# The last attention unit in one tile shape: scores and side products as four products of 64 rows by 32 columns

## The chip, the cores and the metric

One NeuronCore of one Trainium2 chip. The metric is device time in microseconds (us) of one execution; the profile gives one execution, instruction by instruction. TensorE is PE in the profile, its weight loads are PEld; VectorE is DVE, ScalarE is ACT, GpSimd is POOL, SyncE is SP.

## The reference

A transformer block whose layer norms are modulated by a condition vector: 2048 tokens of width 512, attention with 32 heads of width 16 that share one key head and one value head, then a bilinear feed-forward part of width 1792. All in float32.

```python
mod = (silu(c) @ w_mod).reshape(1, 6, 1, 512)
sa, ca, ga, sb, cb, gb = (mod[:, i] for i in range(6))
h = layernorm(x) * (1 + ca) + sa
q, k, v = heads(h @ wq), h @ wk, h @ wv
p = softmax(q @ k.T * 16 ** -0.5)
x = x + ga * (merge(p @ v) @ wo)
h = layernorm(x) * (1 + cb) + sb
x = x + gb * (((h @ w_gate) * (h @ w_up)) @ w_down)
```

## The kernel before

Large products are made of float16 halves: a float32 operand is split into a high and a low part, and three products (high-high, low-high, high-low, `TERMS` in line 487) accumulate in PSUM.

The attention runs in `NU` = 32 units (8 slices of 256 tokens by 4 groups of 8 heads). A unit has `KT` = 16 tiles of 128 keys, and each of them is one turn of `attend` (line 1314). In a turn PE does four score products, each with 51 rows in the array: `qk_exp` (line 667) multiplies a key tile (51 rows by 128 columns, the weights) with 512 columns of queries. `a` says which half of the array's rows is used (0 to 50 or 64 to 114), `p` which two heads. ACT then takes the exponential of each score bank into a tile P. The last score product of a turn may be issued as two of 256 columns (line 680). At the end of a turn `pv` (line 707) multiplies the P tiles of an earlier turn with the values: 32 columns of weights for each of four heads, so that four products stand side by side in the array's columns. For most key tiles P is float32 and the product is issued as two instructions; for three of 16 key tiles (`F16_AT`, line 53) P is split into float16 halves and there are three terms.

In units 0 to 30 `pv` uses all 128 rows. In unit 31 (`NU - 1`) it uses the array's row halves apart, each with an accumulator of its own (lines 716 to 719), so its products are 64 rows by 32 columns, eight side by side; `pv_out` (line 736) adds the two accumulators. `pv` lags by a turn, so the first two turns of unit 31 end with the 128-row `pv` of unit 30.

The turn's remaining array time is filled with halves of other products. A `Group` (line 499) is one PSUM bank that accumulates `n` products of 128 rows; `half` issues one 64-row half of a product, `whole` (used after the last unit) all 128 rows. With two operands (gate and up weights, 256 columns each, `ffn_work` line 918) the second part of a half is kept in `pending`, and `flush` (line 494) issues it after the next score or maximum. While one row half of the array does a score (512 columns), the other does such a side half (256 and 256 columns, or 512 in a down projection). The order in a turn is written out by hand:

```python
MANY = "x1 e0 x1 m0 x1 e0 x1 e0 x1 m0 x1 m0 x1 m0 x1 e0"
```

`x` is a side half, `e` a score, `m` a row maximum's product (`max_mm`, line 600) for a later unit; the digit is the row half and changes with the turn. The maxima are done ahead, and in unit 31 none is left: there `m` is a side half of a second group (line 1358). A side group whose row half changes waits for an exponential of the turn before (lines 534 to 535, `sync`): the first side half of each turn waits for ACT so. After unit 31 come its last `pv`, the normalisation, the output projection and what is left of the feed-forward work, with 128-row products.

Of the kernel before, what the change touches and what calls it, by code (L numbers as in the profile page):

```python
# [23 lines left out]
ST = 256  # L24
NS = S // ST
NC = KC
NU = NS * NC
# [23 lines left out]
Q_BURSTS = {26: 3, 27: 3, 28: 3, 29: 3}  # L51
F16_FROM = 10
F16_AT = ((0, 5, 10), (0,), (0, 5, 10), (0, 5, 10))
P_SHIFT = float(14 * np.log(2.0))

LOW = -3.0e38
SYNC = mybir.DependencyInfo(mybir.DependencyClass.Sync, mybir.DependencyReason.DATA)
# [11 lines left out]
def adaln_mqa_glu_kernel(ctx: ExitStack, tc: tile.TileContext, x_in, wq_in, wk_in, wv_in, wo_in,  # L69
                         wg_in, wu_in, wd_in, c_in, wm_in, out):  # L70
    nc = tc.nc
# [13 lines left out]
    def ps_hold(name="side", shape=(128, 512)):  # L85

        tag, bufs = pool.popleft()
        t = psum.tile(list(shape), F32, name=name, tag=tag, bufs=bufs)
        held[id(t)] = (t, tag, bufs)
        return t  # L90
# [5 lines left out]
    def ps_mx(name="mx", shape=(128, 512)):  # L96
        t = ps_hold(name, shape)
        ps_give(t)
        return t

    def ps_sc():
        return ps_mx("sc")
# [49 lines left out]
    for i in range(3):  # L152
        t = consts.tile([128, 2, 2, ST], F16, name=f"sst{i}")
# [9 lines left out]
    rows = consts.tile([128, 3], F32, name="rows")  # L163
    prow = consts.tile([128, 2], F32, name="prow")
    nc.gpsimd.tensor_tensor(prow[:, 0:1], ident[:, 50:51], ident[:, 114:115], op=OP.add)
    nc.gpsimd.tensor_scalar(prow[:, 1:2], prow[:, 0:1], -P_SHIFT / 32.0, 0.0, op0=OP.mult, op1=OP.add)
    nc.gpsimd.tensor_scalar(prow[:, 0:1], prow[:, 0:1], P_SHIFT / 32.0, 0.0, op0=OP.mult, op1=OP.add)
    nc.gpsimd.memset(sst[2], 0.0)
# [180 lines left out]
    for k in range(KC):  # L349
        for j in range(4):  # L350
            nc.tensor.matmul(pmA[32 * j:32 * j + 32, 0:256], silr[:, k, 0:32], wmA[:, k, 256 * j:256 * j + 256],
                             start=(k == 0), stop=(k == KC - 1))
# [33 lines left out]
    nc.gpsimd.memset(tok, 0.0)  # L386
    kts16 = sorted({k for ks in F16_AT for k in ks})
    v16 = consts.tile([128, 2, len(kts16), 32], F16, name="v16")
# [102 lines left out]
    sync = {"due": False, "exp": None, "before": None, "half": None, "early": False}  # L491
    pending = []

    def flush():
        for f in pending:
            sync.update(due=True, half=f().ins.name)
        pending.clear()

    class Group:

# [5 lines left out]
        def put(self, r0, r1):  # L506
            if self.p is None:
                if self.prepare:
                    self.prepare()
                self.p = ps_hold("side")  # L510
            terms = self.op(self.did[r0])
            start = sum(self.did) == 0
            for r in range(r0, r1):
                self.did[r] += 1
            stop, rows, w = self.ended(), slice(64 * r0, 64 * r1), BT // len(terms)

            def part(c):
                left, right = terms[c]
                return nc.tensor.matmul(self.p[:, c * w:(c + 1) * w], left[rows], right[rows],  # L519
                                        start=start and c == 0, stop=stop and c == len(terms) - 1)  # L520

            if len(terms) > 1 and r1 - r0 == 1:
                pending.append(lambda: part(1))
                return part(0)
            return [part(c) for c in range(len(terms))][0]
# [5 lines left out]
        def half(self, r):  # L531

            mm = self.put(r, r + 1)
            if self.rows not in (None, r):
                tc.add_manual_dep(mm.ins, sync["before"], SYNC)
            self.rows, self.turn = r, now[0]
            sync.update(due=True, half=mm.ins.name)
            if self.ended():
                ended.append(self)

# [61 lines left out]
    def max_mm(u, a, op):  # L602
        kind, p, t, kc = op
        s = sst[u % 3]
        m = ps_sc() if kind == "diff" else ps_mx()
        keys = [kst[:, kc * 512:(kc + 1) * 512]]
        if kind == "diff":
            keys = [kng, kst[:, (kc + 1) * 512:(kc + 2) * 512]]
        for i, w in enumerate(keys):
            nc.tensor.matmul(m, s[64 * a:64 * a + 48, t // 2, p, t % 2 * 128:(t % 2 + 1) * 128], w[64 * a:64 * a + 48, :],  # L610
                             start=(i == 0), stop=(i == len(keys) - 1))
        part = mparts[u][:, a, 4 * (t // 2) + 2 * p + t % 2, kc:kc + 1]
        if kind == "one":
            nc.vector.tensor_reduce(part, m, axis=AX.X, op=OP.max)  # L614
        elif kind == "diff":
            r = rel[a] = work.tile([128, 512], F32, name="rel", tag="x1", bufs=6)
            relus.append(lambda: nc.scalar.activation(r, m, AF.Relu))
        else:
            nc.vector.tensor_tensor_reduce(out=rel[a], in0=m, in1=rel[a], scale=1.0, scalar=LOW, op0=OP.add,
                                           op1=OP.max, accum_out=part)  # L620
# [34 lines left out]
    pd = {}  # L655
    f16s = [KT * u + k for u in range(F16_FROM, NU) for k in F16_AT[u % NC]]
    assert f16s[0] % KT == 0
# [9 lines left out]
    def qk_exp(u, kt, p, a, last=False):  # L667
        s = sst[u % 3]
        v = u * KT + kt
        if v in f16_set:  # L670
            ptl[u, kt, p, a] = p_sets[f16_set[v]][0][:, 2 * a + p]
        else:
            ptl[u, kt, p, a] = work.tile([128, D], F32, name="P", tag="P", bufs=8)
        t = ps_sc()
        keys = kst[64 * a:64 * a + 51, kt * 128:(kt + 1) * 128]
        if pending and last:
            for c in range(2):
                if c:
                    flush()
                nc.tensor.matmul(t[:, c * ST:(c + 1) * ST], keys, s[64 * a:64 * a + 51, c, p, :], start=True, stop=True)  # L680
        else:
            nc.tensor.matmul(t.rearrange("k (c n) -> k c n", c=2), keys, s[64 * a:64 * a + 51, :, p, :],  # L682
                             start=True, stop=True)
        if last and sync["early"]:
            ex = nc.scalar.activation(tok[:, 1:2], tok[:, 0:1], AF.Copy)  # L685
            tc.add_manual_dep(ex.ins, sync["half"], SYNC)
            sync.update(due=False, exp=ex.ins.name)
        ex = nc.scalar.activation(ptl[u, kt, p, a], t, AF.Exp)  # L688
        if sync["due"]:
            sync.update(due=False, exp=ex.ins.name)  # L690
# [518 lines left out]
    NSTEP = 32  # L1209
# [12 lines left out]
    def max_half(a):  # L1222
        n = mstep[a]
        mstep[a] += 1
        if n >= len(flat):
            return
        u, i, last, ops = flat[n]
        max_parts(u)
        for kind, p, t, kc in ops[a]:
            max_mm(u, a, (kind, p, t, kc))  # L1230
        if mstep[1 - a] <= n:
            return
        u, i, last, ops = flat[n]
        if 0 < u < NU - 1 and i == QPRE:
            load_q(u + 1)
        if i == 12:
            max_parts(u + 1)
        if last:
            max_fin(u)
            (_, f, g), = max_rows(u)  # L1240
            later[min(mstep) + 1] = (f, g)
# [13 lines left out]
    now = [0]  # L1255
# [58 lines left out]
    def attend(u, kt):  # L1314
# [28 lines left out]
        for turn in range(2):  # L1343
# [5 lines left out]
            for j, (what, a) in enumerate(order):  # L1349
                if j == len(order) // 2:  # L1350
                    drain_posts()
                    if style is not NO_SIDE:
                        late_max()
                    hooks(u, 2 * (kt + turn))
                    for vj in f16_split.get(u * KT + kt + turn, ()):
                        p_split(*vj)
                a = a if style is NO_SIDE else a ^ turn
                if what == "m" and mstep[a] >= len(flat) and style is MANY:
                    mstep[a] += 1
                    side_half(a, second)  # L1360
                elif what == "m":
                    max_half(a)
                    drain_relus()
                elif what == "v":
                    end_turn(kt + turn)
                elif what == "x":
                    side_half(a)
                    continue
                else:
                    k = count[a] = count.get(a, -1) + 1  # L1370
                    qk_exp(u, kt + (k // 2 if style is MANY else turn), k % 2, a, j == len(order) - 1)
                flush()
# [48 lines left out]
    for g in begun:  # L1421
        for r in range(2):
            while g.did[r] < g.did[1 - r]:
                g.half(r)
                flush()
# [54 lines left out]
```

## Time and profile before

| what | us |
|---|---|
| median of 3 runs | 1639.53 (1637.69 to 1640.58) |
| the profiled execution | 1641.03 |
| its span, first to last instruction | 1639.1 |
| PE busy in the span | 1619.2 (99%) |
| unit 31, first side product to last `pv` | 1480.1 to 1526.7 |

The span is what the traces show; the profiled execution's time is 1.9 us longer, for what lies around it. Starts are us from the span's first instruction. Matmuls are pipelined: a row's duration is longer than the spacing of products that follow each other, so array time is read from starts.

### The profile page before, as it was taken

To read this page: it belongs to the slowest core of one execution; us is meant where nothing else is said; L and a number is where in the kernel's file an instruction comes from. 1 tells how busy PE (TensorE), PEld (TensorE's weight loads), DVE (VectorE), ACT (ScalarE), POOL (GpSimd) and SP (SyncE) were. 2 spreads that over 40 slices of the span, in tenths; PEclk is the share of its full clock that TensorE was granted. 3 is DMA by queue.
4 is the path that set the end of the run, shared out by engine and by line. 5 is a ranking of instruction groups with operands and counts; after the bars stand their busy time and mean duration, and the time that the engine had idled before them with its cause. 6 is when DMAs were issued, how large, how long until landed. Compare 5 with 4: busy or idle time off the path is not lost.

```text
span 1639.1 us, 41286 instructions
## 1 busy us (share of the span) xinstructions
PE 1619.2 (99%) x15993; PEld 747.7 (46%) x15993; DVE 1401.2 (85%) x2434; ACT 1220.8 (74%) x2421; POOL 955.7 (58%) x1316
## 2 busy tenths in 40 slices
PE   9999999999999999999999999999999999999998
PEld 4332333355533555335543455434545345444776
DVE  8999999889999999999999999999999999980211
ACT  6688878888777788778877788777877778877300
POOL 6857537875755566636656466653657556565422
PEclk9899999999999999999999999999999999999999
DMA  7213313342221000100011001100001001100100
GB/s 257 93 57 101 94 63 115 95 125 90 64 70 28 21 20 26 39 32 20 13 32 35 20 19 33 32 26 26 20 25 33 24 18 33 32 15 22 34 14 14
DMA packets 78996, 79.15 MB, mean 48 GB/s; under 512 B 30408, under 2 KB 59340, under 8 KB 78800
## 3 DMA queue, kind: packets, MB, share of 16 engines
q1 hardware_dynamic: 77744, 76.46, 14.9%
q8 instruction: 125, 2.05, 0.5%
q14 instruction: 71, 0.58, 0.1%
q10 hardware_dynamic: 1056, 0.07, 0.0%
HBM read 56.04 MB, written 17.05 MB: 45 GB/s over the span
## 4 chain that ended last, share of the span: by engine, by line
PE 92%; DVE 2%; POOL 2%; ACT 2%; DMA 1%; issue 1%; SPq 0%; POOLq 0%; ACTq 0%; DVEq 0%
PE side L519 41%; PE pv L728 29%; PE mx L610 8%; PE sc L682 8%; PE sc L680 3%; DVE mpart L614 2%; ACT P L688 1%; DMA wmA<-in_w_mod_dram 0%; PE pk L298 0%; PE sc L278 0%; PE part L290 0%; PE mxt L638 0%; DMA kwb<-in_B_w_down_dram 0%; PE sc L610 0%; POOL wg L1175 0%
## 5 line engine op out<-in xcount | busy, mean ns | idle before, releaser
L614 DVE TENSOR_REDUCE mpart<-mx 128x1 f32<-128x512 f32 x2016 | 1272.2, 683 | 83.8 <-PE mx L610 75.7
L688 ACT ACTIVATE P<-sc 128x512 f32<-128x512 f32 x1824 | 982.3, 599 | 219.9 <-PE sc L682 177.7
L610 PE MATMUL mx<-kst,sst 48*128 48x512 f16 x2032 | 628.8, 377 | 3.9 <-ACT P L688 2.6
L682 PE MATMUL sc<-sst,kst 51*128 51x512 f16 x1792 | 597.7, 379 | 0.8 <-ACT P L688 0.3
L519 PE MATMUL side<-h2T,wg 64*128 64x256 f16 (+1 forms) x2396 | 540.5, 271 | 0.6 <-POOL h2T L902 0.3
L519 PE MATMUL side<-h2T,wu 64*128 64x256 f16 (+1 forms) x2396 | 538.2, 270 | 0.0
L728 PE MATMUL pv<-P,vst 128*32 128x512 f32 (+1 forms) x3648 | 485.6, 604 | 0.7
L519 PEld LDWEIGHTS <-wg 64*128 64x128 f16 (+1 forms) x2396 | 226.0, 94 | 220.1 <-ACT P L688 160.4
L519 PE MATMUL side<-wd,glu 64*128 64x512 f16 (+1 forms) x1172 | 271.7, 378 | 0.4 <-ACT tok L685 0.2
L695 POOL TENSOR_TENSOR glu<-glu 128x512 f16<-128x512 f32 x224 | 259.4, 1158 | 18.7
L519 PEld LDWEIGHTS <-wu 64*128 64x128 f16 (+1 forms) x2396 | 226.4, 94 | 42.5 <-issue 5.6
L936 POOL TENSOR_SCALAR glu<-gf 128x256 f16<-128x256 f32 x112 | 45.8, 409 | 278.8 <-DVE gf L935 266.6
L610 PEld LDWEIGHTS <-sst 48*128 48x128 f16 x2064 | 189.8, 94 | 33.0 <-issue 17.8
L694 POOL TENSOR_SCALAR glu<-glu 128x512 f16<-128x512 f32 x224 | 138.4, 618 | 109.7 <-ACT glu L688 79.4
L682 PEld LDWEIGHTS <-kst 51*128 51x128 f16 x1792 | 162.8, 94 | 62.8 <-issue 50.3
L519 PEld LDWEIGHTS <-glu 64*128 64x128 f16 (+1 forms) x1172 | 98.7, 95 | 187.9 <-ACT P L688 69.1
L688 ACT ACTIVATE glu<-sc 128x512 f32<-128x512 f32 x224 | 123.8, 596 | 51.8 <-PE sc L682 50.1
L728 PEld LDWEIGHTS pv<-P,vst 128*32 128x32 f32 (+1 forms) x3648 | 71.9, 107 | 143.6 <-issue 134.3
L935 DVE TENSOR_TENSOR gf<-side,g 128x256 f32<-128x256 f32 x112 | 46.5, 416 | 74.7 <-ACT g L933 64.7
L680 PE MATMUL sc<-sst,kst 51*128 51x256 f16 x512 | 96.9, 268 | 0.0
L519 PE MATMUL side<-h,wq 64*128 64x512 f16 (+1 forms) x372 | 95.0, 376 | 0.4 <-ACT P L688 0.4
L933 ACT ACTIVATE g<-side 128x256 f32<-128x256 f32 x112 | 42.3, 379 | 66.1 <-PE side L519 65.8
(252 smaller groups left out, 1152.4 us busy)
## 6 DMA issues: line engine op xcount, KB each, us to landing
pd<-ev SPq DMA_DIRECT2D x32, 256.0 KB
kwb<-in_B_w_gate_dram SPq DMA_DIRECT2D x32, 224.0 KB
kwb<-in_B_w_up_dram SPq DMA_DIRECT2D x32, 224.0 KB
sst<-qd SPq DMA_DIRECT2D x180, 32.0 KB
qd<-q SPq DMA_DIRECT2D x16, 256.0 KB
oc<-pd SPq DMA_DIRECT2D x64, 64.0 KB
rr<-ri SPq DMA_DIRECT2D x64, 64.0 KB
x<-in_A_x_dram SPq DMA_DIRECT2D x14, 256.0 KB
```

The costliest lines, as they stand in the source:

```text
L519: return nc.tensor.matmul(self.p[:, c * w:(c + 1) * w], left[rows], right[rows], start=start and c == 0, stop=stop and c == len(terms) - 1)
L610: nc.tensor.matmul(m, s[64 * a:64 * a + 48, t // 2, p, t % 2 * 128:(t % 2 + 1) * 128], w[64 * a:64 * a + 48, :], start=(i == 0), stop=(i = ...
L614: nc.vector.tensor_reduce(part, m, axis=AX.X, op=OP.max)
L680: nc.tensor.matmul(t[:, c * ST:(c + 1) * ST], keys, s[64 * a:64 * a + 51, c, p, :], start=True, stop=True)
L682: nc.tensor.matmul(t.rearrange("k (c n) -> k c n", c=2), keys, s[64 * a:64 * a + 51, :, p, :], start=True, stop=True)
L688: ex = nc.scalar.activation(ptl[u, kt, p, a], t, AF.Exp)
L694: nc.gpsimd.tensor_scalar(h[:, j, 0], t[:, j], 1.0, 0.0, op0=OP.mult, op1=OP.add)
L695: nc.gpsimd.tensor_tensor(h[:, j, 1], t[:, j], h[:, j, 0], op=OP.subtract)
L728: nc.tensor.matmul(acc[32 * j:32 * j + 32, :], vt[rows], ps[j][rows], start=start and n == 0, stop=stop and n == len(terms) - 1)
L933: nc.scalar.activation(g, p[:, 0:ST], AF.Copy, scale=2.0 ** -45)
L935: nc.vector.tensor_tensor(gf, p[:, ST:2 * ST], g, op=OP.mult)
L936: nc.gpsimd.tensor_scalar(glu()[:, 0, f, :], gf, 1.0, 0.0, op0=OP.mult, op1=OP.add)
```

## The change

From unit 31 on (`FINE_FROM`), products of one row half are issued as four products with 32 columns of weights each, through a new function `columns`. It is used for score products, for the side halves and for the maxima (of which unit 31 has none). The four use neighbouring quarters of the array's columns and of the PSUM bank's partitions, and all four stream the same right operand. Dependencies that named the one instruction now name the first or the last of the four. `whole` keeps the one product of 128 rows.

```diff
+FINE_FROM = NU - 1
...
     def flush():
         for f in pending:
-            sync.update(due=True, half=f().ins.name)
+            sync.update(due=True, half=f()[-1].ins.name)
         pending.clear()
+
+    def columns(out, left, right, start, stop):
+        if now[0] is None or now[0] < FINE_FROM * NSTEP:
+            return [nc.tensor.matmul(out, left, right, start=start, stop=stop)]
+        return [nc.tensor.matmul(out[32 * j:32 * j + 32], left[:, 32 * j:32 * j + 32], right, start=start, stop=stop)
+                for j in range(4)]
...
             def part(c):
                 left, right = terms[c]
-                return nc.tensor.matmul(self.p[:, c * w:(c + 1) * w], left[rows], right[rows],
-                                        start=start and c == 0, stop=stop and c == len(terms) - 1)
+                mm = nc.tensor.matmul if r1 - r0 == 2 else columns
+                return mm(self.p[:, c * w:(c + 1) * w], left[rows], right[rows],
+                          start=start and c == 0, stop=stop and c == len(terms) - 1)
...
             if self.rows not in (None, r):
-                tc.add_manual_dep(mm.ins, sync["before"], SYNC)
+                tc.add_manual_dep(mm[0].ins, sync["before"], SYNC)
             self.rows, self.turn = r, now[0]
-            sync.update(due=True, half=mm.ins.name)
+            sync.update(due=True, half=mm[-1].ins.name)
...
-                nc.tensor.matmul(t[:, c * ST:(c + 1) * ST], keys, s[64 * a:64 * a + 51, c, p, :], start=True, stop=True)
+                columns(t[:, c * ST:(c + 1) * ST], keys, s[64 * a:64 * a + 51, c, p, :], start=True, stop=True)
         else:
-            nc.tensor.matmul(t.rearrange("k (c n) -> k c n", c=2), keys, s[64 * a:64 * a + 51, :, p, :],
-                             start=True, stop=True)
+            columns(t.rearrange("k (c n) -> k c n", c=2), keys, s[64 * a:64 * a + 51, :, p, :],
+                    start=True, stop=True)
```

The call in `max_mm` (line 610) is replaced in the same way.

## Rows read from the trace of the kernel before

**Rows 1.** The page: busy time by engine; the chain's shares by engine.
```profile
PE 1619.2 (99%) x15993; PEld 747.7 (46%) x15993; DVE 1401.2 (85%) x2434; ACT 1220.8 (74%) x2421; POOL 955.7 (58%) x1316
...
PE 92%; DVE 2%; POOL 2%; ACT 2%; DMA 1%; issue 1%; SPq 0%; POOLq 0%; ACTq 0%; DVEq 0%
```

**Rows 2.** Windows: length, busy PE PEld DVE ACT POOL (x), clock, DMA share, GB/s.
```profile
1480.14:1526.72 46.58, 46.58 (x650) 22.95 (x646) 2.19 (x5) 35.46 (x71) 26.18 (x33) 1.00 0.06 19
...
1524.19:1526.72 2.53, 2.53 (x58) 0.93 (x56) 0.00 (x0) 0.77 (x2) 0.00 (x0) 1.00 0.00 0
...
1512.96:1515.59 2.63, 2.63 (x51) 1.71 (x49) 0.42 (x1) 2.50 (x7) 0.86 (x2) 1.00 0.03 6
```

**Rows 3.** The chain of waits after unit 31: start us, us, what.
```profile
1526.80 26.78 PE side L519 x216
...
1554.45 80.38 PE side L519 x572
```

**Rows 4.** Timeline of PE around a float32 `pv`: start us, us, what.
```profile
1506.92 0.27 PE L680 MATMUL sc<-sst,kst 51*128 51x256 f16 x1
1506.93 0.27 PE L519 MATMUL side<-h2T,wg 64*128 64x256 f16 x1
1507.04 0.27 PE L680 MATMUL sc<-sst,kst 51*128 51x256 f16 x1
...
1507.24 0.63 PE L728 MATMUL pv<-P,vst 64*32 64x512 f32 x4
...
1507.69 0.61 PE L728 MATMUL pv<-P,vst 64*32 64x512 f32 x4
...
1508.26 0.28 PE L519 MATMUL side<-h2T,wg 64*128 64x256 f16 x1
```

**Rows 5.** Timeline of PE, `pv` after `pv` at the unit's end.
```profile
1525.09 0.61 PE L728 MATMUL pv<-P,vst 64*32 64x512 f32 x4
...
1525.52 0.61 PE L728 MATMUL pv<-P,vst 64*32 64x512 f32 x4
...
1525.94 0.40 PE L728 MATMUL pv<-glu,v 64*32 64x512 f16 x4
```

**Rows 6.** Timeline of PE around a float16 `pv`.
```profile
1512.78 0.27 PE L519 MATMUL side<-h2T,wu 64*128 64x256 f16 x1
1512.98 0.40 PE L728 MATMUL pv<-glu,v 64*32 64x512 f16 x4
1512.99 0.40 PE L728 MATMUL pw<-glu,v 64*32 64x512 f16 x4
1513.20 0.39 PE L728 MATMUL pv<-glu,v 64*32 64x512 f16 x4
...
1513.42 0.39 PE L728 MATMUL pv<-glu,v 64*32 64x512 f16 x4
...
1513.75 0.28 PE L519 MATMUL side<-h2T,wg 64*128 64x256 f16 x1
```

**Rows 7.** Timeline of ACT in the turn of rows 4.
```profile
1505.82 2.19 ACT L688 ACTIVATE P<-sc 128x512 f32<-128x512 f32 x4 [0.40 <-PE sc L682]
```

**Rows 8.** Windows of line 519, side products: length, PE (x), PEld (x), clock, DMA.
```profile
1480.14:1494.30 14.16, 9.40 (x59) 3.55 (x61) 1.00 0.09 28
1494.30:1524.10 29.80, 20.56 (x214) 15.10 (x211) 1.00 0.05 17
```

**Rows 9.** Windows of line 682, score products of 512 columns, the same stretches.
```profile
1480.14:1494.30 14.16, 6.90 (x21) 1.97 (x21) 1.00 0.09 28
1494.30:1524.10 29.80, 11.02 (x34) 3.11 (x33) 1.00 0.05 17
```

**Rows 10.** Windows of line 680, score products of 256 columns, the later stretch.
```profile
1494.30:1524.10 29.80, 3.63 (x20) 1.88 (x20) 1.00 0.05 17
```

**Rows 11.** Groups by form, PEld, 1487 to 1527: busy us, mean ns | idle.
```profile
L519 PEld LDWEIGHTS <-wu 64*128 64x128 f16 x86 | 8.1, 94 | 0.7
...
L728 PEld LDWEIGHTS <-v 64*32 64x32 f16 x72 | 0.9, 91 | 1.2 <-issue 1.0
```

**Rows 12.** Timeline of PEld, the loads of the float16 `pv` of rows 6.
```profile
1512.97 0.34 PEld L728 LDWEIGHTS <-v 64*32 64x32 f16 x24 [0.21 <-issue]
```

More of the change, by code (lines that the diff above doesn't have):

```diff
@@ L609, in max_mm @@
         for i, w in enumerate(keys):
-            nc.tensor.matmul(m, s[64 * a:64 * a + 48, t // 2, p, t % 2 * 128:(t % 2 + 1) * 128], w[64 * a:64 * a + 48, :],
-                             start=(i == 0), stop=(i == len(keys) - 1))
+            columns(m, s[64 * a:64 * a + 48, t // 2, p, t % 2 * 128:(t % 2 + 1) * 128], w[64 * a:64 * a + 48, :],
+                    start=(i == 0), stop=(i == len(keys) - 1))
         part = mparts[u][:, a, 4 * (t // 2) + 2 * p + t % 2, kc:kc + 1]
```

## Prediction

> **What bounds the kernel now.** I began with the page: PE is busy for 99% of the span and carries 92% of the chain that ended last [rows 1]. The change acts in one unit alone, so I read that stretch in windows next: unit 31 lasts 46.58 us, PE is busy in all of it at the full granted clock of 1.00, and DVE has next to nothing to do [rows 2]. ACT is the only other engine that is near its limit: in a turn with an extra eviction it is busy 2.50 of 2.63 us [rows 2]. After the unit the chain is PE's side products almost to the end [rows 3], with fixed amounts of work, so what unit 31 gains or loses on PE comes out at the end one for one.
>
> Whether PE's busy time is array time is read from starts. In a turn, products of 64 (or 51) rows by 128 columns with 256 columns streamed follow each other every 0.11 us in each row half (1506.92 to 1507.04 for scores), so 51 rows count as 64 and cost no gap. The gaps lie where `pv` comes in. Its first product starts 0.20 us after the last score product, 0.09 us more than that spacing; and from the second float32 set to the next side product are 0.57 us (1507.69 to 1508.26) [rows 4], where one `pv` set follows another after 0.43 us [rows 5]: 0.14 us more. The float16 `pv` shows the same: 0.20 us on the way in, and 0.33 us on the way out where its sets are 0.22 us apart [rows 6]. So a visit to `pv` and back costs 0.23 us. The type is not the reason, since in [rows 6] it is float16 on both sides and in [rows 5] float32 is followed by float16 without a gap; what changes in both gaps is the tile's shape, 128 columns against 32.
>
> **What the change removes.** With all products of the unit 64 by 32 the gaps go. Turns 2 to 14 have both (11 with a float32 `pv`, 2 with a float16 one), turn 15 the one on the way in. Turns 0 and 1 still end with unit 30's 128-row `pv` and keep theirs, and behind the last `pv` come 128-row products, which keeps that one. At most this is 13 x 0.23 + 0.09 = 3.1 us.
>
> **What is late next.** The first side half of a turn waits for an exponential of the turn before. In the turn shown ACT's fourth exponential ends at 1505.82 + 2.19 = 1508.01 [rows 7], and the side product starts at 1508.26; without the gaps it could start at 1508.03. How long the signal takes from ACT to PE no row shows; the other way, a score product that ends at 1507.31 [rows 4] is followed by an exponential of some 0.55 to 0.60 us that ends at 1508.01, so 0.10 to 0.15 us. With 0 to 0.1 us for it such a turn saves 0.23 to 0.13 us; I take 0.17, between the ends, for the seven float32 turns that end with split scores as this one does. In the other four float32 turns the last score product (512 columns) starts one slot earlier, and behind the float16 `pv` a small ACT instruction gives the signal early, so they save all. That is 7 x 0.17 + 6 x 0.23 + 0.09 = 2.7 us. A turn of 2.63 us with 2.50 us of ACT work [rows 2] can't shrink to 2.40, so I take off 0.1: 2.6 us. The bounds are 1.9 (signal slow and ACT binding in some turns) and 3.1 us.
>
> **What it adds.** The unit has 59 + 214 side products [rows 8], 21 + 34 scores of 512 columns [rows 9] and 20 of 256 [rows 10]: 348, so 1044 products and as many weight loads are added (a few records can be missing). No DMA, eviction or work on another engine is added, and no queue is reordered; the side half's wait moves to the first of four, and behind it on PE stand the same turn's products as before.
>
> *Array time.* Four products side by side must stream like one. In [rows 6] eight of them with 512 columns take 0.22 us a set, as one product of 512 columns does in two slots of 0.11 us, so I put it at nothing. What is different is that four here stream one operand, where `pv` streams four; that asks no more than `pv` does.
>
> *Weight loads.* A 64x32 float16 load takes 91 ns in the mean and a 64x128 one 94 ns [rows 11], and 24 small ones take 0.34 us together [rows 12], so they overlap and one comes to at most 14 ns. Four, 0.06 us, are ready within the 0.11 us of the product before: nothing. The Trainium skill speaks against this: "TensorEngine Tiling (Array Packing)", Restrictions and Gotchas, says that column tiling excludes fast weight load. If for that reason the four loads went one behind another at 91 ns, a product would wait 0.36 us in place of 0.11; the rows agree with the rule only so far as a load of a quarter of the columns is no shorter.
>
> *Handing over the instructions.* This is the cost that the trace does not show. Turns 5 to 15 have 268 products, 24.4 each [rows 8 to 10]; now 98, and 16 of `pv`: 114 pairs of load and product in a turn that takes (1512.98 - 1507.24) / 2 = 2.87 us [rows 4, 6]. Turns 0 to 4 have 80 products [rows 8, 9], 16 each: 64 + 16 = 80 pairs. A pair costs nothing if it is handed over in 2.64 us / 114 = 23 ns, and the heavy turns are slower than now above 2.87 / 114 = 25 ns. The lower bound is in [rows 6]: four pairs start within 0.01 us (1512.98 to 1512.99), 3 ns each, but such a burst may have been waiting ready. The upper bound is the densest longer stretch, 58 products in 2.53 us [rows 2], 44 ns each, in which PE never lacked an instruction. I take the side below 23 ns, since the burst is nearest in kind (the same shape, load and product alternating) and since PE shows no hole anywhere in these rows; it is the weakest step.
>
> **The sum.** 2.6 us off the profiled execution gives 1641.03 - 2.6 = 1638.4. The median of the runs is 1.5 us below that execution; from it, 1639.53 - 2.6 = 1636.9 us, 0.16% less. A measurement of this kernel tells some 0.2% (3.3 us) from no change, so this counts as the same.
>
> **The rivals.**
> 1. *Slower: the instruction stream binds.* PE would wait for its own instructions in turns 5 to 15. For it: the number of pairs per turn grows from 40 to 114, and no long stretch shows over one per 44 ns. Against it: the burst. It decides from 25 ns a pair. At 33 ns, in the middle of what is open, a heavy turn takes 3.76 us, 0.89 more, 11 times, and light turns still gain some 0.7 in all: +9.1, 1648.6 us. At 38 ns it is 1656.5, at 44 ns 23.1 + 3.1 = +26, 1665.7 us.
> 2. *A floor near the break-even.* Pairs at 24 to 27 ns, at which the gaps' gain is given back in the heavy turns: 11 x (114 x 26 ns - 2.87) = +1.0, light turns -0.7: 1639.8 us, no change. The Trainium skill, "TensorE: Matmul & The Clock Gate", The HAM clock gate, gives about 25 ns as the least distance of two matmul starts however small; by that a heavy turn would take 114 x 25 ns = 2.85 us, as now. [rows 6] show starts far closer than that, in different tiles.
> 3. *Faster by over 0.2%.* All 3.1 us, the signal from ACT hidden, and a little more in turns 0 and 1 because the row half's change is cheaper than the column change: 1636.0 us. For it: in [rows 4] the exponential ends 0.02 us before it is needed. Against it: it needs every bound at its good end.
> 4. *The loads go one by one.* Sixteen side products in a row half and turn at 0.36 us are 5.8 us in place of 1.75: some +4 us in each of 16 turns, 1704 us. [rows 12] speak clearly against it.
> 5. *The gaps stay*, because something else than the shape makes them (the turn between accumulators, say): 1639.5 us. [rows 5] change accumulator and type without a gap.
>
> **How the numbers follow.** The forecast has 0.45, rival 1 0.34, rival 2 0.10, rival 3 0.05, rival 4 0.03, rival 5 0.03. Within the forecast a sixth of the chance lies past 0.2%, by the bound of 3.1 us and a measurement that scatters by about as much. Faster: 0.05 + 0.07 = 0.12. Slower: 0.34 + 0.03 and a little of rival 2, 0.38. Same: 0.50. The forecast's own range is 1635.9 to 1638.4. The range given reaches below it by a little of rival 3 and above to 38 ns a pair: 1635.6 to 1657.0. Left out are the upper part of rival 1 (some 0.10), rival 4 and half of rival 3.
>
> **What would show it.** In the changed profile the first `pv` product should start about 0.11 us after the last score product in turns 2 to 15, and the next turn's first side product about 0.43 us after the second float32 set, or up to 0.1 later with ACT named as what ended the wait; a heavy turn should last 2.65 to 2.7 us. Side and score products should come as 64x32 in fours, 0.11 us from four to four in a row half. I am wrong if fours come later than that with no releaser ("issue"), evenly through the heavy turns and less in turns 0 to 4 (rival 1 or 2, and the spacing is the price of a pair); if PEld's busy time grows far past 22.95 us with loads end to end (rival 4); or if the gaps of 0.20 and 0.57 us are still there (rival 5).

## The result, and the profile after

The change made the kernel slower: 1643.61 us (1641.83 to 1645.11, 12 runs) against 1639.40 us (1637.59 to 1640.58, 12 runs), a ratio of 1.0027 with an interval of 1.0018 to 1.0036. The forecast was 1636.9 us, a gain; the time lies inside the range, but on the side of rival 1.

The profiled execution took 1643.3 us (span 1641.3). The turns of unit 31 are of two kinds: turns 0 to 4 are light, with down projections as their only side products, and turns 5 to 15 are dense, with gate and up products as well. First the windows of the changed kernel, with the columns of [rows 2]: the whole of unit 31, the light turns up to the first `pv` set of turn 4, and the rest up to the `pv` at the end of turn 15.

```profile
1479.34:1528.98 49.64, 47.10 (x1688) 27.82 (x1688) 2.18 (x5) 36.13 (x71) 26.24 (x33) 1.00 0.07 21
1479.34:1491.70 12.36, 12.36 (x368) 5.33 (x372) 0.00 (x0) 9.94 (x20) 7.12 (x8) 1.00 0.08 26
1491.70:1526.40 34.70, 32.16 (x1277) 21.20 (x1266) 2.18 (x5) 25.59 (x51) 19.12 (x25) 1.00 0.07 20
```

The unit takes 49.64 us in place of 46.58 [rows 2], and for the first time PE is idle in it: 2.54 us by these rows, more in truth, since a product's row outlasts its array time. (The numbers in brackets count the products and the loads.) No idle time lies in the first stretch, at (368 + 372) / 12.36 = 60 instructions per us; all of it lies in the second, at (1277 + 1266) / 34.70 = 73 per us. Before, the unit ran at (650 + 646) / 46.58 = 28 per us. Single turns say the same. Here are a light one (turn 3) and a dense one (turn 12), first of the changed kernel, then of the kernel before:

```profile
1487.52:1490.22 2.70, 2.70 (x88) 1.18 (x81) 0.00 (x0) 2.54 (x5) 0.77 (x1) 1.00 0.26 97
1513.55:1517.40 3.85, 3.06 (x130) 1.91 (x117) 0.42 (x1) 2.83 (x6) 2.42 (x4) 1.00 0.02 4
```

```profile
1488.45:1491.31 2.86, 2.86 (x40) 0.92 (x32) 0.00 (x0) 2.32 (x5) 0.60 (x1) 1.00 0.24 92
1513.75:1516.62 2.87, 2.87 (x50) 1.64 (x43) 0.42 (x1) 2.48 (x6) 1.80 (x4) 1.00 0.02 6
```

A light turn has become 0.16 us shorter than the 2.86 us it had, the dense one about a microsecond longer. What the dense one looks like inside is in PE's timeline of the changed kernel (start us, us, what, idle time before and what ended it):

```profile
1514.06 0.27 PE L503 MATMUL side<-h2T,wu 64*32 64x256 f16 x1
1514.07 0.39 PE L503 MATMUL sc<-sst,kst 51*32 51x512 f16 x4
1514.10 0.28 PE L503 MATMUL side<-h2T,wu 64*32 64x256 f16 x3
1514.17 0.27 PE L503 MATMUL side<-h2T,wg 64*32 64x256 f16 x1
1515.25 0.28 PE L503 MATMUL side<-h2T,wu 64*32 64x256 f16 x1 [0.79 <-issue]
1515.25 0.29 PE L503 MATMUL side<-h2T,wg 64*32 64x256 f16 x3
1515.26 0.40 PE L503 MATMUL sc<-sst,kst 51*32 51x512 f16 x4
```

Up to 1514.17 the fours come 0.11 us apart, as forecast. Then nothing starts for 1.08 us, and "issue" says that the profile shows nothing that was waited for. After it three groups start within 0.01 us. That is no steady price per pair; it looks as if PE had no instructions, and then many at once. The waits of the changed kernel in unit 31 show how often (us in total, times, longest):

```profile
PEld L503 <- ACT P L696: 8.2, 10, 0.8
...
PEld L503 <- issue: 5.0, 8, 1.1
...
PE side L503 <- issue: 2.0, 5, 0.8
```

The first of these three is the weight loads' wait for ACT at the turns' starts, of which the kernel before had 9.2 us in its unit 31. The pauses without a releaser of the loads for scores and side products are new: before, only loads for `pv` had such, of 0.4 us at the most. The page of the profile names a candidate, the queue that brings the instructions themselves. It had 125 packets and 2.05 MB in the whole execution before; after:

```profile
q8 instruction: 134, 2.20, 0.6%
```

So a packet is 16 KB. PE's 2 x 15993 instructions before [rows 1] are 256 to a packet, and its 2 x 1062 added ones made nine more packets. The DMA view of the changed kernel from 1500 to 1528, cut in 40 slices of 0.7 us, shows when they came:

```profile
GB/s 91 4 12 23 0 0 0 0 23 0 0 0 0 23 0 0 0 0 23 0 0 0 0 23 0 0 0 0 23 0 0 0 0 23 0 0 0 0 23 0
...
q8 instruction: 8, 0.13, 2.0%
```

One packet in every fifth slice, that is in 3.5 us, while the queue takes only 2.0% of the 16 engines' time, some 1.1 us a packet. 256 instructions in 3.5 us are 73 per us, the rate of the dense stretch.

### The profile page after: what moved, and what is told of

Same layout as the page of the kernel before. It is cut to its first block, busy times and chain, and to the rows that moved or that the text cites. A ratio compares the mean times of both kernels' runs of the same rounds, so it can differ in the third digit from the quotient of the medians.

```text
span 1641.3 us, 43412 instructions
## 1 busy us (share of the span) xinstructions
PE 1620.5 (99%) x17055; PEld 755.1 (46%) x17055; DVE 1401.1 (85%) x2434; ACT 1222.2 (74%) x2421; POOL 955.2 (58%) x1316
## 4 chain that ended last, share of the span: by engine, by line
PE 93%; DVE 2%; POOL 2%; ACT 2%; issue 1%; DMA 0%; SPq 0%; POOLq 0%; ACTq 0%; DVEq 0%
PE side L502 33%; PE pv L736 28%; PE sc L502 11%; PE mx L502 8%; PE side L527 7%; PE side L503 2%; DVE mpart L622 2%; ACT P L696 1%; PE misc L180 1%; PE sc L279 0%; PE pk L299 0%; PE part L291 0%; PE mxt L646 0%; PE pw L736 0%; PE sc L503 0%
## 5 line engine op out<-in xcount | busy, mean ns | idle before, releaser
L502 PE MATMUL sc<-sst,kst 51*128 51x512 f16 (+1 forms) x2230 | 672.9, 354 | 0.9 <-ACT P L696 0.3
L502 PE MATMUL side<-h2T,wg 64*128 64x256 f16 x2016 | 456.5, 270 | 0.6 <-POOL h2T L910 0.3
L502 PE MATMUL side<-h2T,wu 64*128 64x256 f16 x2016 | 454.3, 269 | 0.0
L502 PEld LDWEIGHTS <-wg 64*128 64x128 f16 x2016 | 189.2, 94 | 207.1 <-ACT P L696 154.5
L502 PEld LDWEIGHTS <-kst 51*128 51x128 f16 x2230 | 203.9, 94 | 65.4 <-issue 50.3
L502 PE MATMUL side<-wd,glu 64*128 64x512 f16 x896 | 211.6, 377 | 0.4 <-ACT tok L693 0.2
L502 PEld LDWEIGHTS <-wu 64*128 64x128 f16 x2016 | 189.6, 94 | 36.7 <-issue 4.4
L502 PEld LDWEIGHTS <-glu 64*128 64x128 f16 x896 | 74.3, 94 | 159.9 <-ACT P L696 65.7
L502 PE MATMUL side<-h,wq 64*128 64x512 f16 x360 | 91.7, 376 | 0.4 <-ACT P L696 0.4
L502 PE MATMUL side<-wo,och 64*128 64x512 f16 x336 | 80.8, 377 | 0.0
```

What stands on the lines that cost most here:

```text
L502: return [nc.tensor.matmul(out, left, right, start=start, stop=stop)]
```

## The experiments

**Theories.** F: PE's instructions arrive in blocks of 256, one block in some 3.5 us at the most, and the changed unit wants more. H: every pair of load and product takes a fixed time to hand over, some 27 ns. W: the dense turns are slow by themselves (the array; the four column quarters, which run apart in time; ACT's signal). Each run below was compared with the kernel before on its own chip.

**Extra products alone** (e1). Kernel before, with

```diff
+    stream = ps_hold("stream")
+    for n, w in ((640, 32), (64, 512), (640, 128), (64, 512), (640, 32)):
+        for i in range(n):
+            j = 32 * (i % 4)
+            nc.tensor.matmul(stream[j:j + 32, 0:w], kst[0:64, j:j + 32], kst[0:64, 512:512 + w], start=True, stop=True)
+    ps_give(stream)
```

> The kernel before, with five stretches of products behind the last P times V of unit 31, into a bank of their own: 640 products of 64 rows by 32 columns with 32 columns streamed, 64 with 512, 640 with 128, 64 with 512, 640 with 32, four column quarters in turn; they are extra work and feed nothing. Theory F (PE's instructions arrive in blocks of 256, one block in some 3.5 us at the most): after the first few hundred instructions the stretches of 32 and of 128 streamed columns run at the same 27 ns per pair of load and product, in dense bursts with pauses of over 1 us with no releaser, some 17 us per stretch less what lay ready; the stretches of 512 at 54 ns per pair without pauses. Rival H (each pair takes some 27 ns to hand over): the same mean, but evenly spaced, no pause of over 0.2 us. Rival W (the array or the weight loads are the limit): the 128-column stretch at 13.5 ns a pair or a multiple of the 32-column one, no pauses. Added time: F and H 50 to 58 us, W 25 us.

Measured: 1703.93 us in a single run, 64 more than before. PE's timeline of the first stretch, and the DMA view from 1529.4 to 1540 in slices of 0.27 us:

```profile
1525.57 1.78 PE L1423 MATMUL stream<-kst 64*32 64x32 f16 x185
1529.41 1.19 PE L1423 MATMUL stream<-kst 64*32 64x32 f16 x128 [2.06 <-issue]
1532.89 1.22 PE L1423 MATMUL stream<-kst 64*32 64x32 f16 x128 [2.29 <-issue]
1536.37 1.23 PE L1423 MATMUL stream<-kst 64*32 64x32 f16 x128 [2.25 <-issue]
```

```profile
GB/s 0 0 0 0 62 0 0 0 0 0 0 0 0 0 0 0 0 62 0 0 0 0 0 0 0 0 0 0 0 0 62 0 0 0 0 0 0 0 0 0
```

128 products with their 128 loads, 256 instructions, start together, run in 1.2 us and are followed by more than 2 us of nothing; the bursts are 3.48 us apart each time, and to each belongs one packet of 16 KB. This is F. H is out: within a burst a pair takes under 10 ns. Ahead of the first pause 185 pairs ran, 370 instructions, so something over one block lay ready. The 128-column stretch tells nothing, because the granted clock fell during these bursts; the windows from burst to burst and of a piece of that stretch are

```profile
1529.41:1532.89 3.48, 1.19 (x129) 1.09 (x129) 0.00 (x0) 0.00 (x0) 0.00 (x0) 0.75 0.02 5
1532.89:1536.37 3.48, 1.23 (x130) 1.12 (x130) 0.00 (x0) 0.00 (x0) 0.00 (x0) 0.50 0.02 5
...
1550.00:1564.00 14.00, 14.00 (x536) 14.00 (x532) 0.00 (x0) 0.00 (x0) 0.00 (x0) 0.50 0.02 5
```

With the granted clock at 0.50 (1.2 GHz) four 128-column products need as long as four of 256 columns at 1.00, some 0.11 us or 27 ns each, and 14.00 / 536 = 26.1 ns is what they took: the array's bound and the blocks' happen to be equal there. The lower clock also made each stretch of 64 products with 512 columns last 6.8 us in place of 64 x 54 ns = 3.5; that is most of what the measured 64 us has over F's 50 to 58.

**The same with wider products** (e7), stretches of 640 with 320 and 640 with 192 columns.

> The kernel before with two stretches of extra products behind the last P times V, 64 rows by 32 columns, four column quarters in turn: 640 with 320 columns streamed, then 640 with 192. By the array (four side by side, 2.4 GHz) a block of 128 pairs would take 4.3 us and 2.6 us. Theory F: the 320 stretch is bound by the array, 33 ns a pair and no pause; the 192 stretch by the blocks, 27 ns a pair in the mean with a pause of about 0.9 us in each 3.5 us, however, only after the instructions that lay ready are used up. Rival H: 33 and 27 ns, evenly. If the clock falls to 1.2 GHz, both stretches are bound by the array and tell nothing of 27 ns.

Measured: 1679.99 us in a single run. PE's timeline, whose first row merges the 320-column products with the first 313 of 192; windows in the first stretch, of the first burst and behind the start of the last one; and the DMA view from 1546 to 1564 in slices of 0.45 us:

```profile
1524.58 28.41 PE L1423 MATMUL stream<-kst 64*32 64x320 f16 x953
1553.63 2.82 PE L1423 MATMUL stream<-kst 64*32 64x192 f16 x128 [0.64 <-issue]
1557.11 2.82 PE L1423 MATMUL stream<-kst 64*32 64x192 f16 x128 [0.66 <-issue]
1560.86 2.93 PE L1423 MATMUL stream<-kst 64*32 64x192 f16 x71 [0.94 <-issue]
```

```profile
1526.00:1545.00 19.00, 19.00 (x568) 15.80 (x564) 0.21 (x1) 0.00 (x0) 0.00 (x0) 1.00 0.06 18
1553.60:1557.10 3.50, 2.82 (x128) 2.59 (x128) 0.00 (x0) 0.00 (x0) 0.00 (x0) 1.00 0.02 5
1560.80:1565.00 4.20, 4.14 (x78) 3.42 (x79) 0.00 (x0) 0.00 (x0) 0.00 (x0) 0.53 0.01 4
```

```profile
GB/s 0 0 0 0 36 0 0 0 0 0 0 36 0 0 0 0 0 0 0 36 0 0 0 0 0 0 0 36 0 0 0 0 0 0 0 0 36 0 0 0
```

The 320-column products run without a pause (568 in 19.00 us, 33 ns each, at full clock). The 192-column ones go on without one for a while, then again 128 pairs at a time, 3.48 and 3.75 us apart, though the array needs only 2.6 us for them. So the limit is a number of instructions per time, and it holds at full clock.

The two DMA views show a little of where the 3.48 us go. In both runs a packet is moved some 1.1 us after a burst began, and the next burst begins 2.3 to 2.6 us after that packet's start, whether the burst lasts 1.2 us (e1) or 2.8 us (e7). So the blocks come one at a time, at a distance that neither PE's work nor the transfer of some 1 us sets.

**New shape in every second dense turn** (e2):

```diff
+FINE_TURNS = (2, 3, 4, 5, 7, 9, 11, 13, 15)
...
-        if now[0] is None or now[0] < FINE_FROM * NSTEP:
+        if now[0] is None or now[0] < FINE_FROM * NSTEP or now[0] % NSTEP // 2 not in FINE_TURNS:
```

> The changed kernel with the new shape in turns 2 to 5, 7, 9, 11, 13 and 15 of unit 31 alone. Theory F: 114 and 41 pairs in turn are some 55 instructions per us, below the 73 per us of a block in 3.5 us, so no pause of over 0.3 us without a releaser, each new-shape turn 2.70 us in place of 2.87, in sum 1.3 us faster than before. Rival H: a single dense turn is covered by what is queued, also 1.3 us faster. Rival W (the dense turns are slow by themselves: array, skew of the quarters, ACT's signal): each of the five dense ones loses 0.3 us as the mean one of the full change did, in sum about 1 us slower than before.

Turns 0, 1, 6, 8, 10, 12 and 14 keep the old shape. Measured: 1638.47 us, ratio 0.9991 (0.9983 to 1.0000), 1.3 us faster, as F and H had it; the slower time that W expected lies outside the interval. Unit 31 in its windows, and its dense turn 9 in the new shape:

```profile
1480.06:1524.77 44.71, 44.71 (x1217) 26.14 (x1217) 2.18 (x5) 35.59 (x71) 26.24 (x33) 1.00 0.07 22
```

```profile
1504.29:1507.05 2.76, 2.76 (x125) 1.92 (x118) 0.42 (x1) 2.34 (x5) 1.82 (x4) 1.00 0.00 0
```

At 54 instructions per us PE is never idle, and a whole dense turn with all four quarters takes 2.76 us, less than the 2.87 it had. That speaks against W.

**Two turns of three** (e3): `FINE_TURNS = (2, 3, 4, 5, 6, 7, 9, 10, 12, 13, 15)`.

> The new shape in turns 2 to 7, 9, 10, 12, 13 and 15 of unit 31. Theory F: some 66 instructions per us in the dense part, just below 73: no pause or one short one (under 0.4 us) where two dense turns follow each other, 1.7 us faster than before. Rival H: 228 pairs at 27 ns less some 30 queued are 5.3 us for two turns that last 5.4, also 1.7 us faster, without pauses. Rival W: 0.3 us lost in each of seven dense turns, about 1.6 us slower than before.

Measured: 1640.10 us, ratio 1.0002 (0.9993 to 1.0011), no gain. F was right in kind and wrong in size: the unit takes 46.04 us, and in PE's timeline there is one pause without a releaser, longer than expected, in turn 7:

```profile
1500.18 0.28 PE L504 MATMUL side<-h2T,wu 64*32 64x256 f16 x1 [1.02 <-issue]
```

Turn 7 is the third dense turn in a row, since turn 5 is dense as well and the expectation counted it with the light ones: turns 5 and 6 take 242 + 244 instructions in 5.07 us (1492.84 to 1497.91), 96 per us, where the expectation had a mean of 66. Nor do the other pairs gain: their second turns, 10 and 13, last 2.88 and 2.99 us, no less than before.

**The same with the early ACT signal** (e4):

```diff
-            sync["early"] = u * KT + kt + turn - 1 in f16_set
+            sync["early"] = u * KT + kt + turn - 1 in f16_set or u == NU - 1
```

> As the run with two turns of three, and the small ACT copy that gives the first side half its signal before the last exponential is issued in every turn of unit 31, not only in those with a float16 P times V. If the wait for ACT is what keeps the float32 turns at 2.70 us and not 2.64: the gap from the second float32 set to the next side product falls from 0.50 to 0.43 us in new-shape turns, and the whole is 0.7 us faster than that run, 2.4 us faster than before. If ACT binds by its busy time, the copy's 0.2 us per turn delay the exponentials and the turns stay at 2.70 us or grow.

Measured: 1640.09 us, ratio 1.0001 (0.9992 to 1.0010), the same as e3. The gap itself does go. The changed kernel's timeline at the end of light turn 3, and this kernel's near the end of light turn 3:

```profile
1489.68 0.60 PE L736 MATMUL pv<-P,vst 64*32 64x512 f32 x4
...
1490.22 0.40 PE L503 MATMUL side<-wd,glu 64*32 64x512 f16 x4
```

```profile
1490.46 0.59 PE L737 MATMUL pw<-P,vst 64*32 64x512 f32 x3
...
1490.88 0.38 PE L504 MATMUL side<-wd,glu 64*32 64x512 f16 x3
```

0.54 us from the second set to the next side product became 0.42, a set's own length. The unit was 0.5 us shorter than in e3 (45.52 us), too little for the runs' time to show.

**All turns, but half of the side products' quarters** (e5). Most side halves issue two of their four quarters, so half of the side products' output columns in unit 31 are left out and the kernel computes less. The shape and the time that the array streams stay:

```diff
+    def columns(out, left, right, start, stop, quarters=4):
...
+                for j in range(quarters)]
...
+                if mm is columns and not (start or stop):
+                    return columns(self.p[:, c * w:(c + 1) * w], left[rows], right[rows], False, False, 2)
```

> The changed kernel in all 16 turns of unit 31, but the side halves there issue only the first two of the four column quarters, except the first and the last product of a group: half of the side products' output columns in unit 31 are left out, the shape, the streamed columns and the order stay. Theory F: some 79 pairs a dense turn are 59 instructions per us, below 73, so the pauses without a releaser go, every dense turn takes about 2.70 us, and the whole is about 2.1 us faster than before (6 us faster than the full change). Rival W (shape, skew or ACT make dense turns slow): array time and ACT's work are the same, so dense turns keep most of their 0.3 us and the whole stays slower than before.

Measured: 1636.88 us, ratio 0.9982 (0.9973 to 0.9991), 2.8 us faster than before. Its unit, and a dense turn in it:

```profile
1478.42:1522.51 44.09, 44.09 (x1174) 26.50 (x1172) 2.19 (x5) 35.55 (x71) 26.27 (x33) 1.00 0.07 22
```

```profile
1505.05:1507.76 2.71, 2.71 (x80) 1.77 (x77) 0.00 (x0) 2.14 (x4) 2.54 (x4) 1.00 0.02 6
```

All 16 turns have the new shape and the array streams as many columns as in the full change, but at 53 instructions per us the pauses are gone and the dense turn takes 2.71 us. By itself this would leave a form of W in which four quarters at work are slower than two; but in e2 a dense turn with all four took 2.76 us. Together the two decide against W. e5 also splits the full change: 46.58 - 44.09 = 2.5 us gained by the shape, 49.64 - 44.09 = 5.6 us lost to missing instructions.

**The full change with the early signal** (e6).

> The full change, with the small ACT copy that gives the first side half's signal early in every turn of unit 31. Theory F: the dense turns' length is set by 256 instructions in 3.5 us, so an earlier signal only moves the wait into the pauses; light turns gain 0.1 us each, and the whole is 0 to 0.6 us faster than the full change, that is 3.6 to 4.2 us slower than before. Rival W in its form with ACT: the 0.5 us gaps behind P times V go and the whole is 1 us or more faster than the full change.

Measured: 1642.49 us, ratio 1.0018 (1.0009 to 1.0027), 2.8 us slower than before, less than the 3.6 to 4.2 expected (the interval is 1.5 to 4.4). Against the full change, each by its own reference, that is 1.4 us faster, which taken alone would fit rival W; but the two intervals overlap, and the time can't decide. The profile does: the unit takes 49.45 us against 49.64, as F expects, and the loads' wait moved from ACT to missing instructions in the waits of unit 31 (7.5 us in place of 5.0):

```profile
PEld L504 <- issue: 7.5, 14, 1.1
PEld L504 <- ACT tok L694: 4.1, 11, 0.4
```

**Spread, with and without the signal** (e8, e9): `FINE_TURNS = (2, 3, 4, 5, 7, 9, 10, 12, 13, 15)`, e8 with e4's edit.

> The new shape in turns 2 to 5, 7, 9, 10, 12, 13 and 15 of unit 31, and the early ACT signal in all turns of the unit. Theory F: with a coarse turn 6 the light turns are not followed by two dense ones, so the pause of 1.3 us of the run with two turns of three does not come (at most one under 0.4 us); 1.8 to 2.2 us faster than before. Rival W: seven dense or half-dense turns lose 0.3 us each, slower than before.

> The run with the shape spread over turns 2 to 5, 7, 9, 10, 12, 13 and 15, without the early ACT signal. If the signal is worth 0.1 us in each new-shape turn that isn't bound by blocks, this is 0.5 to 0.9 us slower than with it: 0.9 to 1.5 us faster than before. If the order of the turns alone made the gain, it equals the run with the signal, 1.8 us faster than before.

Measured: e8 1637.90 us, ratio 0.9988 (0.9980 to 0.9997), 1.8 us faster than before and, each by its own reference, 6.0 faster than the full change; e9 1639.18 us, ratio 0.9993 (0.9984 to 1.0002), 0.5 us faster, short of both values expected, though its interval takes them in. Unit 31 of e8 has no idle time by PE's rows, but its turn 13 is long:

```profile
1478.10:1523.07 44.97, 44.97 (x1293) 27.09 (x1293) 2.19 (x5) 36.60 (x84) 26.23 (x33) 1.00 0.07 22
```

```profile
1512.46:1516.04 3.58, 3.58 (x124) 1.96 (x109) 0.00 (x0) 2.38 (x6) 3.24 (x5) 1.00 0.02 5
```

Turn 13 is the second new-shape turn in a row; it took 2.87 us before. A pause hides in it: the loads for `pw`, the products of `pv` in the other row half, wait 0.7 us without a releaser in the middle of a set, while the rows of products already issued cover the time. In e9 the same turn takes 3.85 us and the wait is 1.0 us. So the expectation of at most one pause under 0.4 us did not hold: of the two pairs of dense turns in a row, 9 and 10 pass (turn 10 of e8 takes 2.74 us), 12 and 13 do not.

**Every second turn with the signal** (e10): e2 with e4's edit.

> The new shape in turns 2 to 5, 7, 9, 11, 13 and 15, with the early ACT signal. Theory F: no pauses, each new-shape turn shorter by up to 0.1 us than without the signal: 1.6 to 2.1 us faster than before, against 1.3 without it.

Measured: 1638.26 us, ratio 0.9991 (0.9982 to 1.0000), against e2's 0.9991: 1.5 us faster than before, just short of the 1.6 to 2.1 expected and not to be told from e2. The signal made the unit shorter wherever it was added: 46.04 to 45.52 us (e3, e4), 49.64 to 49.45 (the full change, e6), 45.94 to 44.97 (e9, e8), 44.71 to 44.43 (e2, e10), one profile each. The runs' times can't tell these. Of the complete kernels only e8 is faster than the one before by an interval that leaves out 1; e2 and e10 can't be told from it, and what the signal adds in time stays open.

## Why the prediction was wrong

*What bounds the kernel, and the gaps.* Right. The gaps are the price of changing the tile's shape: in e5, which has all turns in the new shape and no pause, the unit became 2.5 us shorter, and the forecast had 2.6. The gap's length in [rows 4] and [rows 6], 0.23 us for a visit, was read correctly. On the way in the changed kernel has 0.10 us in place of 0.20:

```profile
1506.30 0.27 PE L503 MATMUL sc<-sst,kst 51*32 51x256 f16 x3
1506.40 0.59 PE L736 MATMUL pv<-P,vst 64*32 64x512 f32 x2
```

On the way out e4 has 0.42 us in place of 0.57.

*What is late next.* The mechanism was right, its extent was not. The prediction let four float32 turns (2, 3, 4 and 7), whose last score product has 512 columns, escape the wait for ACT. They wait too: light turn 3 has 0.54 us behind the second set in place of 0.43, and saves 0.16 us and not 0.23. That is 4 x 0.07 = 0.3 us of the sum, which would then be 2.3 us; e5's 2.5 lies between.

*Array time and weight loads.* Right. Four products with one operand follow four others after 0.11 us, and the loads of 32 columns overlap:

```profile
L503 PEld LDWEIGHTS <-wu 64*32 64x32 f16 x339 | 10.5, 92 | 3.8 <-issue 3.2
```

This group of the changed kernel, by form, has a mean of 92 ns against 94 for the large load [rows 11], but in the first full burst of e1 129 loads keep PEld busy for 1.09 us, 8 ns each, below the forecast's 14. In the unit PEld's busy time rose from 22.95 to 27.82 us only, with four times the loads for scores and side products. Rival 4 did not come.

*Handing over the instructions.* This is the step that failed: "I take the side below 23 ns, since the burst is nearest in kind". The term was put at nothing. The burst in [rows 6] was the pace of instructions that had already arrived; e1 has a pace of that kind, under 10 ns a pair, inside each block. The sustained supply is 256 instructions in 3.48 us, 27 ns a pair, which lies between the bounds of 3 and 44 ns and just past the 25 ns at which the dense turns turn slower; it cost the unit 5.6 us. Weighing a burst of a few products against a long stretch was the mistake: a store that is refilled slowly looks infinitely fast until it is empty. The prediction had the numbers to be wary, for 114 pairs in 2.64 us are 86 instructions per us against 28 before.

*The rivals.* Rival 1 came, at a price between its own and that of rival 2: 5.6 us lost against 2.5 gained is 3.1 us in the unit, and the runs show 4.2; what makes the difference is not shown. Its mechanism, evenly later fours, was not what happened, and the sign given for it ("evenly through the heavy turns") would have missed the pauses; "issue" and "less in turns 0 to 4" were right. Rival 2's figure of 11 x 0.1 us was for 26 ns; at the measured 27.2 ns its formula gives 11 x (114 x 27.2 ns - 2.87) = 2.5 us, less 0.7 in the light turns. In the profile the dense turns lost some 3.5 us (3.06 in the unit and 0.5 gained in light turns 2 to 4), so 1 us of it is not accounted for by the mean pace. The Trainium skill, "TensorE: Matmul & The Clock Gate", was cited there for 25 ns between starts; e1's bursts are closer than that, in different column quarters, so it is not that floor which bound.

A page that the prediction did not draw on bears on this case. The Trainium skill, "Runtime: NRT & Kernel Launch", Instruction fetch mechanics, says that instructions come in blocks of 16 KB (256) which the sequencer fetches itself while it runs the block before. The trace agrees with the size (134 packets, 2.20 MB). The page adds that this is hidden because the sequencer needs some 20 cycles per instruction; here it is not hidden, since 256 instructions ran in 1.2 us and the next ones began 3.48 us after they had begun.

What stays open is what fills the 3.5 us of a block beside the 1 us of its packet, and whether other traffic changes that; no run varied it.

## What to carry to other kernels

Splitting a product into four to spare TensorE a change of tile shape (0.23 us for a visit here) multiplies its instructions, loads included, and here they arrived at no more than 73 per us over more than a block or two; count instructions per us in the densest stretch, turn by turn and not on average, and read the instruction queue's packets beside it. A pause on PE with "issue" as its releaser and a burst behind it is the sign that the blocks bind; look at the turns' lengths and at the weight loads' waits too, since PE's busy rows can hide such a pause (e8). What took the pauses away here was fewer instructions per time: with new and old shape in alternation no pause was left (e2), and 1.3 to 1.8 us of the forecast's 2.6 were gained (e2, e8).

## What was not expected of the hardware

Three things. Over longer stretches PE got no more than 256 instructions in some 3.5 us (3.48 in e1 and e7, 3.5 in the changed kernel). It ran such a block in 1.2 us where the products were small (e1). And the granted clock came down in both runs with extra products: from 1.00 to 0.50 in e1, with bursts of 1.2 us and pauses of over 2 us, and to 0.53 in the window behind 1560.80 in e7, after two bursts of 2.8 us and pauses of only 0.6 to 0.9 us. In unit 31 of the changed kernel, with pauses of up to 1.1 us, it stayed at 1.00. These rows give no rule for it.
